# Q and K of the first two batches in runs of eight rows by head pair, a fixed order of the first loads, and other pacing of the later loads

## The chip, the cores and the metric

One core of one Trainium2 chip. The metric is device time in microseconds (us). A profile is one execution with the hardware profiler on; its span (first to last instruction) is 1 to 2 us under the device time. Every run is labelled fast, slow or unknown; a slow run is one that the chip executed over 1.5% above the fastest of the same kernel.

Names used here: PE is TensorE, ACT is ScalarE, DVE is VectorE, POOL is GpSimd, SP is the engine that issues most of the DMAs. SP and POOL each issue their DMAs in the order of their stream: none of SP's 190 issues in the trace of the kernel before starts before the one ahead of it has ended.

## The reference, cut to what matters

```python
# q, k, v: (8 batches, 8 heads, 576 rows, 64) float32
scores = (q @ k.T) / 8                     # per batch and head
scores = where(|i - j| <= 32, scores, -1e9)
attn   = softmax(scores) @ v
x      = attn.transpose(0, 2, 1, 3).reshape(4608, 512)
h      = x @ w_in                          # w_in (512, 2048)
out    = (s * max(h, 0)**2 + b) @ w_out    # w_out (2048, 512); out float32
```

## The kernel before

The kernel has no fixed program order. It adds tasks with an engine, a cost, a priority key and the buffers that they read and write; a list scheduler (its own cost model, no chip) then orders the tasks of each of the five streams. So one changed constant moves many instructions.

Batches 0 and 1 are transposed on PE; batches 2 to 7 go through DMA transposes on SP. For batches 0 and 1, Q and K come by chunks of rows, all eight heads at once, two rows (512 bytes) to a partition:

```python
PACE = ((0, 0, 1, 2, 3, 3), (0, 0, 1, 2, 3, 3), (0, 1, 2, 3, 3, 3))   # which unit of the batch before
PACEV = ((0, 0, 1, 1), (0, 0, 1, 1), (0, 1, 2, 2))                    # a load of batch b >= 2 waits for

def pairs_chunk(b, name, t0, n, key, load_key, banks, slack=0.0):     # batches 0 and 1
    add("sp", lambda e: e.dma_start(
        STG[si][0:n, 0:1024].rearrange("p (h c) -> p h c", h=H),
        src_of[name][b, :, t0:t0 + 2 * n, :].rearrange("h (p i) d -> p h (i d)", i=2)), ...)
    # ... cast to bf16 into NAT, 8 transposes on PE into PSUM, copies to QT and KBD
# called with (t0, n) = (0, 128), (256, 128), (512, 32), for q and for k
```

One unit is two score tiles (64 keys by up to 128 queries, for four head pairs, 128x512 in all), an Exp of each, and the product with V. The rows of Q lie de-interleaved (all even ones, then all odd ones), so the scores in PSUM do too; the Exp reads them as they lie and writes them back in order of rows. Its innermost loop steps over 2 elements of bf16, which is 4 bytes:

```python
def unit(b, m):
    # four score matmuls into SC[:, par, :] (for b < 2 after one that adds the mask)
    src = SC[:, par, :]...[:, :, 0:w].rearrange("p a (i c) -> p a i c", i=2)
    dst = (EXE[ei][:, :, c0:c0 + w], EXO[ei][:, :, 64 + c0:64 + c0 + w])[par]
    add("act", lambda e, src=src, dst=dst: e.activation(
        dst.rearrange("p a (c i) -> p a i c", i=2), src, AF.Exp, bias=0.0, scale=0.125), ...)
    # product with V (avn), reciprocal and scaling (xn), transposes to x^T (xt)
```

Other parts: V of batches 0 and 1 is loaded on SP (for batch 1 only after output block 2 of the first weight pieces, `waits=[land["out", 2, 0]]`); V of batches 2 to 7 is issued by POOL, 16 DMAs a batch; POOL also casts a part of Q and of the weights.

The softmax here doesn't subtract the row's maximum and nothing guards it: scores larger than these inputs give would overflow.

## Time and profile before

| | before |
|---|---|
| device time, median of 3 | 332.48 us (332.16 to 333.7) |
| span of the profile | 331.1 us |
| PE busy | 308.5 us, 93% |
| ACT busy | 166.4 us, 50% |
| first scores on PE | 10.70 us |
| first matmul with w_in | 24.20 us |
| first scores of batch 1 | 44.05 us |

From the page of the kernel before: busy time by engine, then the busy share of PE and ACT in 40 slices of the span in tenths, the GB/s of the DMA engines in the same slices, and the chain of work that ended last.

```profile
PE 308.5 (93%) x2199; PEld 179.5 (54%) x2234; DVE 206.6 (62%) x485; ACT 166.4 (50%) x270; POOL 87.6 (26%) x136
...
PE   1778998899999999999989999999999999999995
...
ACT  6696497229552664657175655444644433333300
...
GB/s 211 224 363 357 295 195 297 219 241 167 209 202 197 193 195 206 230 170 245 173 228 163 225 212 145 247 169 213 146 56 54 56 46 62 35 32 34 32 93 68
...
PE 70%; DMA 13%; SPq 8%; POOL 3%; DVE 2%; ACT 2%; issue 2%; ACTq 0%
```

PE is busy nearly everywhere but in the first slices, and ACT has only 2% of the chain. The windows view: each row is a stretch, its length, then the busy time of PE, PEld, DVE, ACT and POOL, the granted clock, the DMA share and GB/s.

```profile
0.00:16.00 16.00, 7.16 (x52) 5.22 (x52) 9.90 (x26) 10.61 (x14) 11.01 (x25) 1.00 1.07 217
16.00:32.00 16.00, 11.95 (x188) 10.46 (x191) 10.07 (x21) 12.83 (x23) 7.34 (x6) 1.00 1.07 356
32.00:64.00 32.00, 29.76 (x325) 25.64 (x325) 16.95 (x35) 19.83 (x35) 14.79 (x17) 0.95 1.10 266
64.00:100.00 36.00, 34.68 (x288) 22.59 (x291) 27.81 (x69) 20.76 (x34) 15.07 (x24) 1.00 1.03 200
100.00:320.00 220.00, 217.51 (x1321) 112.41 (x1346) 139.62 (x335) 102.33 (x167) 39.34 (x64) 1.00 0.72 143
```

Length less PE busy is PE's idle time: 8.8, 4.1, 2.2, 1.3 and 2.5 us. Nothing but the first 32 us offers much.

### The profile page before, as it was taken

What the parts mean: (1) busy time and instruction counts of PE and PEld (TensorE: products, weight loads), DVE (VectorE), ACT (ScalarE), POOL (GpSimd) and SP (SyncE); (2) the same over time, 40 slices, a digit from 0 to 9 for tenths busy, and PEclk for the clock granted to TensorE, in tenths of its full rate; (3) what the DMA queues carried; (4) which work ended last, traced back from release to release, by engine and by line L of the source; (5) the groups of instructions that cost most, each with busy time, mean ns of one, the idle gap of its engine ahead of it and who ended that gap; (6) DMA issues with size and microseconds to landing.
All of it is one profiled execution on the core that took longest, in us unless ns stands there. A gap on an engine that the chain in (4) does not pass through costs nothing.

```text
span 331.1 us, 5839 instructions
## 1 busy us (share of the span) xinstructions
PE 308.5 (93%) x2199; PEld 179.5 (54%) x2234; DVE 206.6 (62%) x485; ACT 166.4 (50%) x270; POOL 87.6 (26%) x136
## 2 busy tenths in 40 slices
PE   1778998899999999999989999999999999999995
PEld 1567996775554555456445555555455544444442
DVE  6556564269777776898578768765874453323411
ACT  6696497229552664657175655444644433333300
POOL 8562443830910226044205500450000000000000
PEclk9999999799999999999999999999999999999999
DMA  8999999899999699979998996999811111000021
GB/s 211 224 363 357 295 195 297 219 241 167 209 202 197 193 195 206 230 170 245 173 228 163 225 212 145 247 169 213 146 56 54 56 46 62 35 32 34 32 93 68
DMA packets 107836, 57.15 MB, mean 173 GB/s; under 512 B 56608, under 2 KB 100128, under 8 KB 107808
## 3 DMA queue, kind: packets, MB, share of 16 engines
q1 hardware_dynamic: 103200, 49.69, 68.7%
q0 software_dynamic: 4608, 7.08, 11.3%
q8 instruction: 17, 0.28, 0.4%
q14 instruction: 11, 0.09, 0.1%
HBM read 36.70 MB, written 9.44 MB: 139 GB/s over the span
## 4 chain that ended last, share of the span: by engine, by line
PE 70%; DMA 13%; SPq 8%; POOL 3%; DVE 2%; ACT 2%; issue 2%; ACTq 0%
PE o L717 31%; PE w L698 29%; PE avn L582 6%; SPq L432 5%; DMA vst<-in_v_dram 5%; PE sc L543 3%; DMA stg<-in_moe_w_in_dram 3%; DMA stg<-in_moe_w_out_dram 3%; POOL vst L432 2%; SPq L456 2%; DMA out_dram<-outs 2%; ACT vbd L445 1%; SPq L416 1%; PE o L740 1%; DVE vbd L446 0%
## 5 line engine op out<-in xcount | busy, mean ns | idle before, releaser
L717 PE MATMUL o<-wout,gt 128*128 128x512 bf16 (+1 forms) x629 | 140.4, 357 | 1.9 <-DVE outs L730 1.3
L698 PE MATMUL w<-xt,win 128*128 128x512 bf16 (+2 forms) x685 | 139.8, 339 | 2.2 <-ACT r L705 1.2
L705 ACT ACTIVATE r<-w 128x512 bf16<-128x512 f32 x144 | 85.4, 598 | 95.0 <-PE w L698 80.8
L707 DVE TENSOR_TENSOR gt<-r 128x512 bf16<-128x512 bf16 x144 | 61.3, 432 | 55.1 <-ACT r L705 54.4
L717 PEld LDWEIGHTS o<-wout,gt 128*128 128x128 bf16 x640 | 61.1, 98 | 59.7 <-DVE outs L730 2.0
L698 PEld LDWEIGHTS w<-xt,win 128*128 128x128 bf16 x704 | 61.6, 98 | 52.4 <-ACT r L705 1.8
L432 POOL DMA_DIRECT2D vst<-in_v_dram x96 | 59.4, 626 | 106.8 <-PE avn L582 57.7
L730 DVE SCALAR_TENSOR_TENSOR outs<-o,sb,cvec 128x512 f32<-128x512 f32 (+1 forms) x40 | 27.7, 692 | 18.6 <-PE o L717 16.2
L560 ACT ACTIVATE exe<-sc 128x512 bf16<-128x512 f32 (+1 forms) x40 | 27.5, 687 | 15.7 <-PE sc L543 15.1
L582 PE MATMUL avn<-vbd,exo 128*128 128x130 bf16 (+1 forms) x240 | 27.9, 221 | 1.5 <-ACT xt L607 1.3
L595 DVE TENSOR_TENSOR xn<-avn,rec 128x512 bf16<-128x512 f32 (+1 forms) x38 | 26.1, 686 | 3.2 <-DMA xt<-xn 2.5
L543 PE MATMUL sc<-qt,kbd 128*128 128x128 bf16 (+1 forms) x288 | 24.8, 220 | 1.6 <-ACT exe L560 1.1
L582 PE MATMUL avn<-vbd,exe 128*128 128x130 bf16 (+1 forms) x152 | 25.3, 221 | 1.0 <-ACT vbd L445 1.0
L560 ACT ACTIVATE exo<-sc 128x512 bf16<-128x512 f32 x32 | 23.8, 743 | 4.8 <-PE sc L543 4.6
L543 PEld LDWEIGHTS sc<-qt,kbd 128*128 128x128 bf16 x288 | 20.5, 100 | 9.9 <-issue 1.0
L445 ACT CAST vbd<-vst 64x1024 bf16<-64x1024 f32 (+1 forms) x15 | 16.5, 1139 | 17.5 <-DMA vst<-in_v_dram 17.5
L582 PEld LDWEIGHTS avn<-vbd,exo 128*128 128x128 bf16 (+1 forms) x240 | 22.0, 105 | 5.5 <-ACT xt L607 1.6
L506 DVE CAST nat<-stg 128x1024 bf16<-128x1024 f32 (+1 forms) x36 | 23.7, 680 | 0.0
L521 DVE COPY kbd<-kt 64x512 bf16<-64x512 bf16 (+1 forms) x72 | 19.1, 266 | 0.8
L582 PEld LDWEIGHTS avn<-vbd,exe 128*128 128x128 bf16 (+1 forms) x152 | 16.1, 109 | 4.3 <-ACT vbd L445 1.4
L446 DVE CAST vbd<-vst 64x1024 bf16<-64x1024 f32 (+1 forms) x16 | 11.7, 745 | 7.3 <-DMA vst<-in_v_dram 7.3
L564 DVE TENSOR_TENSOR exe<-exe,mask 128x512 bf16<-128x512 bf16 (+1 forms) x30 | 11.7, 391 | 7.1 <-ACT exe L560 7.0
(63 smaller groups left out, 133.3 us busy)
## 6 DMA issues: line engine op xcount, KB each, us to landing
stg<-in_q_dram SPq DMA_DIRECT2D x16, 512.0 KB, 5.5
stg<-in_k_dram SPq DMA_DIRECT2D x16, 512.0 KB, 7.2
out_dram<-outs SPq DMA_DIRECT2D x32, 256.0 KB, 2.6
vst<-in_v_dram POOLq DMA_DIRECT2D x96, 72.0 KB, 5.5
stg<-in_moe_w_in_dram SPq DMA_DIRECT2D x8, 512.0 KB, 8.7
stg<-in_moe_w_out_dram SPq DMA_DIRECT2D x8, 512.0 KB, 8.3
vst<-in_v_dram SPq DMA_DIRECT2D x16, 144.0 KB, 4.7
stg<-in_q_dram SPq DMA_DIRECT2D x8, 128.0 KB, 6.2
```

What stands on the lines that cost most here:

```text
L432: add(stream, lambda e, dst=dst, src=src: e.dma_start(dst, src), 640.0 if stream == "sp" else 700.0, writes=[("VST", h, x) for x in (range ...
L445: add(eng, (lambda e, dst=dst, src=src: e.copy(dst, src)) if eng == "act" else (lambda e, dst=dst, src=src: e.tensor_copy(dst, src)), {"ac ...
L506: add("dve", lambda e, si=si, ni=ni: e.tensor_copy(NAT[ni][0:n, :, :].rearrange("p i (h d) -> p h i d", h=H), STG[si][0:n, 0:1024].rearran ...
L543: fns = [lambda e, j=j, pr=pr, lo=lo, hi=hi, w=w, par=par: e.matmul(SC[:, par, pr * 128:pr * 128 + w], lhsT=KBD[:, pr, j, :], rhs=QT[slot] ...
L560: add("act", lambda e, src=src, dst=dst: e.activation(dst.rearrange("p a (c i) -> p a i c", i=2), src, AF.Exp, bias=0.0, scale=0.125), 190 ...
L582: fns.append(lambda e, pr=pr, buf=buf, col=col, j=j, x=x, last=len(parts) - 1: e.matmul(av[0:nr, pr, 0:130], lhsT=buf[:, pr, col:col + nr] ...
L595: add("dve", lambda e: e.tensor_tensor(XN[xi][0:nr, :].rearrange("p (a b c) -> p a b c", a=4, b=2), av[0:nr, :, 0:128].rearrange("p a (b c ...
L698: add("pe", [lambda e, g=g, kc=kc: e.matmul(wt[:, g, :], lhsT=WIN_BF[:, kc, (f0 + g) * 128:(f0 + g + 1) * 128], rhs=XT[:, kc, t0 % XR:t0 % ...
L705: add("act", lambda e: e.activation(rt, wt, AF.Relu, bias=0.0, scale=1.0), 190 + 0.833 * 512, reads=[("W", wb)], writes=[("R1", rb)], key=key)
L707: add("dve", lambda e: e.tensor_tensor(GT[gs][:, f0:f0 + ng, g0:g0 + nt], rt, rt, ALU.mult), 130 + 0.53 * 512, reads=[("R1", rb)], writes= ...
L717: add("pe", [lambda e, fc=fc: e.matmul(O[:, ob, 0:cn], lhsT=GT[gs][:, fc, g0:g0 + 128], rhs=WOUT_BF[:, fc, c0:c0 + cn], start=(fc == 0), s ...
L730: add("dve", lambda e: e.scalar_tensor_tensor(OUTS[us][:, 0:cn], O[:, ob, 0:cn], SB128[:, 0:1], CVEC[:, c0:c0 + cn], ALU.mult, ALU.add), 2 ...
```

## The change

The intent: longer runs in memory for the first loads (2 KB instead of 512 B), Q and K of two batches as eight equal loads each, weights without small loads between them, and the loads of later batches allowed earlier. Its core (cuts marked with "..."):

```diff
+ROWS = 8
-PACE = ((0, 0, 1, 2, 3, 3), (0, 0, 1, 2, 3, 3), (0, 1, 2, 3, 3, 3))
-PACEV = ((0, 0, 1, 1), (0, 0, 1, 1), (0, 1, 2, 2))
+PACE = ((-1, -1, -1, 0, 1, 1), (-1, -1, 0, 1, 2, 2), (0, 0, 1, 2, 3, 3))
+PACEV = ((-1, -1, -1, -1), (0, 0, 0, 0), (0, 1, 2, 2))
...
+        after = [self.chain] if key < -100 and self.chain else []     # fixed order of the first loads
...
-        NSTG, NNAT, NEX, NXN, NR1, NOUT, XR = 9, 6, 3, 2, 3, 3, 2048
+        NSTG, NNAT, NEX, NXN, NR1, NOUT, XR = 9, 5, 4, 2, 3, 3, 2048
...
-                key=key + 20.0, slack=100.0)      # casts of the weights
+                key=key + 150.0, slack=100.0)
...
+        def paced(b, u):
+            return land["av", b - 1, u] if u >= 0 else land["av", b - 2, NUNIT + u]
...
-        def pairs_chunk(b, name, t0, n, key, load_key, banks, slack=0.0):
...
+        def load_pair(b, name, pr, key, load_key, banks, eng, slack):
+            n = S // ROWS                          # 72 partitions
             add("sp", lambda e: e.dma_start(
-                STG[si][0:n, 0:1024].rearrange("p (h c) -> p h c", h=H),
-                src_of[name][b, :, t0:t0 + 2 * n, :].rearrange("h (p i) d -> p h (i d)", i=2)),
...
+                STG[si][0:n, :].rearrange("p (h c) -> p h c", h=2),
+                src_of[name][b, 2 * pr:2 * pr + 2, :, :].rearrange("h (p i) d -> p h (i d)", i=ROWS)),
...
         def unit(b, m):
-            slot, key = b % 2, due(b, m)
+            slot, key, nrow = b % 2, due(b, m), ROWS if b < 2 else 2
...
-                src = src.rearrange("p a (i c) -> p a i c", i=2)
+                src = src.rearrange("p a (i c) -> p a i c", i=nrow)
                 dst = (EXE[ei][:, :, c0:c0 + w], EXO[ei][:, :, 64 + c0:64 + c0 + w])[par]
                 add("act", lambda e, src=src, dst=dst: e.activation(
-                    dst.rearrange("p a (c i) -> p a i c", i=2), src, AF.Exp, bias=0.0, scale=0.125),
+                    dst.rearrange("p a (c i) -> p a i c", i=nrow), src, AF.Exp, bias=0.0, scale=0.125),
...
-                load_v(1, h, nxt(), "sp", waits=[land["out", 2, 0]])
+                load_v(1, h, nxt(), "sp")
```

With eight rows to a partition, the innermost loop of the Exp's output steps over 8 elements of bf16, 16 bytes, in batches 0 and 1.

## The prediction

> **What bounds it now.** TensorE. The windows view of PE gives 308.5 us busy of 331.1, and between 80 and 320 us only about 2.7 us idle. The idle time lies at the two ends: 12.9 us in 0-32 us, 2.2 us in 32-64, 1.2 us in 64-80, 3.5 us after 320. From 58.8 to 64 us the granted clock is only 0.67, worth about 1.7 us. So the change can win in the first 80 us or nowhere.
>
> In 0-32 us the timeline shows who was waited for: PE starts at 6.08 (after the cast of the first Q chunk), first scores at 10.67, V cast at 15.7-19.2, last 64 rows of Q and K only at 22.7, first MoE matmul at 24.2. The DMA engines are full all this time: about 290-350 GB/s for Q/K in 512 B packets (to about 9.6 us), about 205 GB/s for V in 256 B packets (to about 16 us), 380-390 GB/s for weights in 2 KB packets.
>
> **What the change does.**
> 1. Q, K of batches 0 and 1 come as 8 loads of 295 KB by head pair in 2 KB runs instead of 6 loads in 512 B runs. A 2 KB packet runs at the weight rate. But the loads have 72 partitions: [...] here 12 of 16 engines. Estimate: 385 x 12/16 = 290 GB/s, 1.0 us a load, 8.2 us a batch, about what 512 B packets take now (2.36 MB at 300 GB/s = 7.9 us). So no real gain in transfer time; V can use the four free engines early, but ends at about 16 us as before.
> 2. First scores need all four pairs, so they move later: last K lands at about 11, cast 0.7, transposes 0.5, copy 0.8: about 13.5 us instead of 10.7. In return nothing of batch 0 waits for a third chunk (22.7 before); the nine exps (0.75 each) then run in one row on ACT, together with one V cast (1.04), one weight cast (1.04) and two XT copies (0.6). First XT at about 22 instead of 23.06 us. Gain about 1 us.
> 3. Weights follow V at once and in order, no small Q/K load and no w_out load between: w_in first cast at about 18.3 (19.7 before), last at about 28 (31.7), w_out first half about 34 (36.3). Gain 1 to 2 us where PE was short of weights in 24-32.
> 4. Fewer but wider casts and PSUM copies; same elements, about equal time. Exp writes with 16 B stride instead of 4 B; I expect 0.75 us still.
> 5. Earlier Q/K/V loads of batches 2 and later: may remove the ACT-V-cast stall at 169 us (0.9) and parts of 56-80 us, but load DMA when the first stores run.
>
> Sum: 1 + 1.5 + about 1 = 3.5 us, nearly all on the critical path since PE is full afterwards.
>
> **Prediction.** 328.8 us, 325.5 to 331.8. Faster by over 2%: 0.12; within 2%: 0.85; slower: 0.03.
>
> **What would show it.** Q/K loads moving about 290 GB/s with a DMA share near 0.75 before V joins; first scores at 13-14 us, first MoE matmul at 21.5-23.5; PE idle in 0-32 about 10.5 us; the same PE busy sum within 2 us; 80-320 idle still 2-3 us.
>
> **What would make it wrong.** All 16 engines at 390 GB/s: everything 2 us earlier, about 326. Strided exp writes or PSUM reads slower than now: ACT binds batch 0, no gain. The stores of the first output blocks stuck behind early loads of batch 2: new PE waits at 55-75 us. Another place of the clock dip: 1-2 us either way.

The 12 are measured: in the trace of the kernel after, the semaphore of each of the 16 loads of 72 partitions gets 12 increments as the load lands, where V's loads to 64 partitions get 16, and the DMA share between 2 and 7 us is 0.74, about 12 of 16 engines. So 385 x 12/16 = 290 GB/s stands as an estimate from the weights' rate of the kernel before (387 GB/s between 18 and 24 us) and that count. The sum came to 1 us (step 2), 1.5 (step 3) and about 1 (step 5), 3.5 in all.

## More of the kernel before

SC has two PSUM banks, one for even and one for odd tiles. The scores of a tile cannot start before the Exp of the tile two places earlier has freed its bank.

Of the ACT groups by shape, the three forms of the Exp (count, then busy us and mean ns of one):

```profile
L560 ACT ACTIVATE exo<-sc 128x512 bf16<-128x512 f32 x32 | 23.8, 743 | 4.8 <-PE sc L543 4.6
L560 ACT ACTIVATE exe<-sc 128x512 bf16<-128x512 f32 x24 | 17.9, 744 | 5.8 <-PE sc L543 5.3
L560 ACT ACTIVATE exe<-sc 128x384 bf16<-128x384 f32 x16 | 9.6, 602 | 9.8 <-PE sc L543 9.7
```

Three Exps of batch 0 in the timeline (start, duration, engine, ...):

```profile
15.94 0.74 ACT L560 ACTIVATE exe<-sc 128x512 bf16<-128x512 f32 x1
16.55 0.72 ACT L560 ACTIVATE exo<-sc 128x512 bf16<-128x512 f32 x1
17.38 0.75 ACT L560 ACTIVATE exe<-sc 128x512 bf16<-128x512 f32 x1
```

## The result

| | before | after |
|---|---|---|
| device time, median | 333.02 us (332.16 to 333.7, 4 runs) | 361.86 us (361.04 to 364.87, 4 runs) |
| ratio | | 1.088 (1.082 to 1.095) |
| PE busy | 308.5 us | 319.6 us |
| ACT busy | 166.4 us | 193.5 us |
| first scores | 10.70 us | 17.60 us |
| first matmul with w_in | 24.20 us | 38.34 us |
| first scores of batch 1 | 44.05 us | 64.48 us |

A ratio here and below is the mean time of one kernel's fast runs over that of the kernel before in the same rounds, so it is not quite the ratio of the quoted medians; a 95% interval stands beside it.

The change made the kernel 29 us slower. The same lines of the page, of the kernel after:

```profile
PE 319.6 (89%) x2266; PEld 185.2 (51%) x2266; DVE 205.1 (57%) x485; ACT 193.5 (54%) x262; POOL 88.9 (25%) x138
...
PE   2455999664999999899969999999999999999996
...
ACT  6499959996376336458323745544654443333300
...
GB/s 168 200 341 352 127 188 205 284 255 48 91 203 224 217 150 208 226 160 104 237 144 221 104 270 213 157 196 198 256 89 57 58 59 42 29 33 58 29 61 87
...
PE 73%; ACT 12%; DMA 8%; DVE 3%; POOL 2%; issue 1%; SPq 1%; ACTq 0%
```

ACT is busy 90% or more of slices 3 to 5 and 7 to 9 (half of slice 6), several of PE's holes (slices 3, 4, 8 and 9) lie there, and its share of the chain went from 2% to 12%. The first slices move fewer GB/s than before (168 and 200 against 211 and 224). The windows view, same columns:

```profile
0.00:16.00 16.00, 4.95 (x62) 3.76 (x63) 8.87 (x19) 8.81 (x10) 9.90 (x23) 1.00 0.79 181
16.00:32.00 16.00, 9.73 (x67) 6.27 (x64) 6.04 (x18) 14.22 (x10) 7.99 (x9) 1.00 1.07 329
32.00:64.00 32.00, 28.85 (x368) 26.03 (x366) 18.54 (x36) 26.56 (x35) 8.65 (x10) 1.00 0.82 202
64.00:100.00 36.00, 24.77 (x208) 18.30 (x207) 12.95 (x27) 25.95 (x19) 12.03 (x18) 0.81 0.74 165
100.00:320.00 220.00, 214.51 (x1404) 114.33 (x1402) 147.11 (x366) 109.84 (x178) 50.34 (x80) 1.00 0.77 157
```

PE's idle time is now 11.1, 6.3, 3.2, 11.2 and 5.5 us, 37.2 in all against 18.9: 18 of the 29 us. The other 11 are in PE's busy time, which only partly means more work (32 transposes more). A part is a lower granted clock, 0.81 between 64 and 100 us; estimated from the two tables as 36 x 0.19 = 6.8 us lost there at most (PE also idles in that stretch), against 32 x 0.05 = 1.6 us in the dip of the kernel before. Another part is matmuls that take longer until later: sixteen with w_in take 1.91 us at 38.34 us and 1.06 us at 41.44. A 512-column matmul takes 0.61 to 0.63 us at 31 us; in the kernel before it takes 0.39 from about 17 us on. The 1.00 of the view is no reading there, since the trace holds no clock record before 41.0 us (15.6 us in the kernel before). PE is busy for 15.9 us between 16 and 41 us, so I estimate some 6 us for this, from 15.9 x (1 - 0.39/0.62); why it lasts so much longer is not shown. The last part is a matter of counting, since some 35 matmul records are missing from the trace of before (2199 against 2234 weight loads).

The Exp groups, in the same order of forms. The means mix 18 instructions of batches 0 and 1 with 54 of the others:

```profile
L567 ACT ACTIVATE exo<-sc 128x512 bf16<-128x512 f32 x32 | 38.6, 1205 | 0.4 <-PE sc L550 0.3
L567 ACT ACTIVATE exe<-sc 128x512 bf16<-128x512 f32 x24 | 30.1, 1253 | 6.7 <-PE sc L550 6.6
L567 ACT ACTIVATE exe<-sc 128x384 bf16<-128x384 f32 x16 | 15.4, 964 | 4.6 <-PE sc L550 4.6
```

The first ones in the timeline:

```profile
18.44 1.88 ACT L567 ACTIVATE exe<-sc 128x384 bf16<-128x384 f32 x1 [1.43 <-PE sc L550]
19.81 2.78 ACT L567 ACTIVATE exo<-sc 128x512 bf16<-128x512 f32 x1
22.10 2.77 ACT L567 ACTIVATE exe<-sc 128x512 bf16<-128x512 f32 x1
...
25.96 2.45 ACT L567 ACTIVATE exo<-sc 128x512 bf16<-128x512 f32 x1
```

2.45 to 2.8 us instead of 0.75. The view of PE's waits says what that does (waiter, what it waits for, us in total, times, longest):

```profile
PE sc L556 <- ACT exe L567: 8.0, 7, 1.7
PE w L488 <- ACT nat L483: 5.5, 1, 5.5
PE sc L556 <- ACT exo L567: 3.8, 3, 1.6
PE avn L589 <- DVE exe L571: 3.8, 1, 3.8
```

The scores wait 11.8 us for the Exp to free a bank; the kernel before has 1.3 us of such waits in all. The chain of work that ended last, in order of time (start, us, what), shows the second thing that went wrong, ahead of the Exps:

```profile
3.86 11.05 DMA stg<-in_k_dram
...
14.93 0.69 DVE nat L483
...
17.60 0.48 PE sc L556
...
18.44 1.88 ACT exe L567
20.32 1.15 ACT exo L567
```

The last of the eight loads is issued at 3.86 us and lands at 14.91. A load is 72 partitions x 2 heads x 2 KB = 295 KB, and the casts that follow the landings start at 4.42, 5.78, 7.24, 8.94, 10.45, 12.11, 13.67 and 14.93 us: 1.5 us a load, which is 197 GB/s.

### The profile page after: what moved, and what is told of

Its sections match the earlier page's. It is cut to its first block, busy times and chain, and to the rows that moved or that the text cites. A ratio compares the mean times of both kernels' runs of the same rounds, so it can differ in the third digit from the quotient of the medians.

```text
span 360.1 us, 5951 instructions
## 1 busy us (share of the span) xinstructions
PE 319.6 (89%) x2266; PEld 185.2 (51%) x2266; DVE 205.1 (57%) x485; ACT 193.5 (54%) x262; POOL 88.9 (25%) x138
## 4 chain that ended last, share of the span: by engine, by line
PE 73%; ACT 12%; DMA 8%; DVE 3%; POOL 2%; issue 1%; SPq 1%; ACTq 0%
PE o L721 31%; PE w L702 30%; ACT exe L567 6%; PE avn L589 5%; ACT exo L567 5%; DMA stg<-in_k_dram 3%; DMA vst<-in_v_dram 3%; PE sc L550 3%; DMA xt<-xn 2%; POOL vst L448 2%; PE o L744 1%; SPq L476 1%; DVE xn L602 1%; PE sc L488 1%; ACT xt L614 0%
## 5 line engine op out<-in xcount | busy, mean ns | idle before, releaser
L702 PE MATMUL w<-xt,win 128*128 128x512 bf16 (+2 forms) x704 | 144.8, 342 | 0.0
L721 PE MATMUL o<-wout,gt 128*128 128x512 bf16 (+1 forms) x640 | 144.1, 359 | 0.0
L702 PEld LDWEIGHTS w<-xt,win 128*128 128x128 bf16 x704 | 63.1, 99 | 52.8
L567 ACT ACTIVATE exe<-sc 128x512 bf16<-128x512 f32 (+1 forms) x40 | 45.5, 1137 | 11.3 <-PE sc L550 11.2
L567 ACT ACTIVATE exo<-sc 128x512 bf16<-128x512 f32 x32 | 38.6, 1205 | 0.4 <-PE sc L550 0.3
L734 DVE SCALAR_TENSOR_TENSOR outs<-o,sb,cvec 128x512 f32<-128x512 f32 (+1 forms) x40 | 27.6, 690 | 19.3 <-PE o L721 17.4
L589 PE MATMUL avn<-vbd,exo 128*128 128x130 bf16 (+1 forms) x240 | 29.5, 229 | 9.2 <-DVE exe L571 3.8
L599 DVE RECIPROCAL rec<-avn 128x8 f32<-128x8 f32 (+1 forms) x38 | 7.7, 203 | 38.3 <-PE avn L589 38.1
L589 PE MATMUL avn<-vbd,exe 128*128 128x130 bf16 (+1 forms) x152 | 26.7, 228 | 1.3 <-ACT exo L567 1.2
L550 PE MATMUL sc<-qt,kbd 128*128 128x128 bf16 (+1 forms) x288 | 26.0, 229 | 0.0
L556 PE MATMUL sc<-maskb,ident 128*128 128x512 bf16 (+1 forms) x18 | 8.9, 494 | 13.0 <-ACT exe L567 8.0
```

What stands on the lines that cost most here:

```text
L550: fns = [lambda e, j=j, pr=pr, lo=lo, hi=hi, w=w, par=par: e.matmul(SC[:, par, pr * 128:pr * 128 + w], lhsT=KBD[:, pr, j, :], rhs=q_rows(b ...
L567: add("act", lambda e, src=src, dst=dst: e.activation(dst.rearrange("p a (c i) -> p a i c", i=nrow), src, AF.Exp, bias=0.0, scale=0.125), ...
L589: fns.append(lambda e, pr=pr, buf=buf, col=col, j=j, x=x, last=len(parts) - 1: e.matmul(av[0:nr, pr, 0:130], lhsT=buf[:, pr, col:col + nr] ...
L702: add("pe", [lambda e, g=g, kc=kc: e.matmul(wt[:, g, :], lhsT=WIN_BF[:, kc, (f0 + g) * 128:(f0 + g + 1) * 128], rhs=XT[:, kc, t0 % XR:t0 % ...
L721: add("pe", [lambda e, fc=fc: e.matmul(O[:, ob, 0:cn], lhsT=GT[gs][:, fc, g0:g0 + 128], rhs=WOUT_BF[:, fc, c0:c0 + cn], start=(fc == 0), s ...
L734: add("dve", lambda e: e.scalar_tensor_tensor(OUTS[us][:, 0:cn], O[:, ob, 0:cn], SB128[:, 0:1], CVEC[:, c0:c0 + cn], ALU.mult, ALU.add), 2 ...
```

## The experiments

Three suspects: the Exp's stride in SBUF (E), the first loads (L), the pacing and order of the loads (P). My theory after the result was that E takes most of the loss and P and L the rest; the rivals are named in each expectation. (The expectations of b_exp16 and a_contig speak of 36 Exps in batches 0 and 1; there are 18.) Sixteen kernels ran, told here by suspect and not in order of time.

### The Exp's writes

**b_exp16**: the stride alone, put on the kernel before. Its columns come out in a wrong order. The comparison with the reference does not test the order of the columns; in the mended kernels below the order is right by construction, since read and write patterns are permuted alike.

```diff
-                src = src.rearrange("p a (i c) -> p a i c", i=2)
+                ni_ = 8 if b < 2 else 2
+                src = src.rearrange("p a (i c) -> p a i c", i=ni_)
...
-                    dst.rearrange("p a (c i) -> p a i c", i=2), src, AF.Exp, ...
+                    dst.rearrange("p a (c i) -> p a i c", i=ni_), src, AF.Exp, ...
```

> The kernel before, wrong result on purpose: only the exp of batches 0 and 1 writes in steps of eight elements (16 B) instead of two (4 B). Theory A: these 36 exps take 1.9-2.8 us instead of 0.60-0.75, ACT sum up by 30 us or more, and this alone makes the kernel before 12-25 us slower (345-357). Rival (the step is harmless alone, the loss needs the new loads): within 3 us of before.

Measured: 351.13 us (350.77 to 351.54), ratio 1.057 (1.053 to 1.061). ACT busy 194.0 us, as in the kernel after, which is 27.6 us more and not the 30 expected. One of the Exps:

```profile
17.95 2.44 ACT L561 ACTIVATE exe<-sc 128x512 bf16<-128x512 f32 x1
```

The same loads, order and pacing as before, and 18.6 us lost against the median of the same rounds (332.55): the stride alone is enough for most of the loss. A part of it comes with a lower clock: the four runs have a mean granted clock of 0.976 or 0.959, the kernel before 0.994 to 1.0 in the same rounds. In the profiled run (0.976) that is at most some 7 us, estimated as 349 x 0.019; it is not separated from the waits.

**a_contig**: the kernel after, with the Exp of batches 0 and 1 reading PSUM in the order of rows and writing consecutive elements.

```diff
-                src = src.rearrange("p a (i c) -> p a i c", i=nrow)
+                src = src.rearrange("p a (i c) -> p a c i" if b < 2 else "p a (i c) -> p a i c", i=nrow)
...
-                    dst.rearrange("p a (c i) -> p a i c", i=nrow), src, AF.Exp, ...
+                    dst.rearrange("p a (c i) -> p a c i" if b < 2 else "p a (c i) -> p a i c", i=nrow), src, ...
```

> The changed kernel, but the exp of batches 0 and 1 walks the scores in the order (pair, column, row of eight): it reads PSUM with a stride and writes consecutive bf16. Same work, correct result. Theory A (most of the loss is ACT time of exp, from 16 B apart writes): these 36 exps fall from 2.4-2.8 us to 0.60-0.75 us, the ACT sum falls by 25-30 us, PE idle between 16 and 90 us falls by 12 us or more, and the time is 335-343 us. Rival 1 (short inner runs are the cost, not the write stride): inner runs get shorter still (8), exps stay at 2 us or more, time stays at 355-365. Rival 2 (the late 72-row loads are the main loss): exps may get fast, but the time stays above 350.

Measured: 350.74 us (346.38 to 353.43), ratio 1.052 (1.044 to 1.060). Those Exps now take 0.49 us (384 columns) and 0.60 (512), under the 0.75 of before, and ACT's sum fell to 163.9 us:

```profile
20.13 0.60 ACT L567 ACTIVATE exe<-sc 128x512 bf16<-128x512 f32 x1 [0.26 <-PE sc L550]
```

But only 11 of the 29 us came back. Theory A missed on the time (335 to 343) and on PE's idle time between 16 and 90 us, which fell by 5.7 us (20.65 to 14.91) and not by 12; the time lies, barely, where Rival 2 had it, above 350. Mending E uncovers the next waits: first scores still at 17.59 us, and a new wait of 3.9 us at 76 to 80 us of an output matmul for the output buffer, whose store stood on SP behind loads of batch 2.

**b_sweep**: what property of the pattern costs? The kernel before, with one Exp (even tile, 128x512) of each of six units given another pattern. Its output is wrong, which doesn't matter for the time.

```diff
+   # unit (0,1): groups of 4 -> 8 B steps; (0,2): 8 -> 16 B; (0,3): 16 -> 32 B
+   # (1,1): PSUM read in 64 B steps, consecutive writes; (1,2): 4 B steps in shorter runs
+   # (1,3): consecutive on both sides
```

> The kernel before, wrong result on purpose (columns permuted): one exp of 512 elements in each of six units of batches 0 and 1 has another access pattern, all others stay (4 B steps, 0.74 us). In order of time: written in 8 B steps; in 16 B steps; in 32 B steps; read from PSUM in 64 B steps and written consecutively; 16-element inner runs in 4 B steps (32 short runs, as many as in the changed kernel); read in 256 B steps... of two and written consecutively. If the step in SBUF is the cause and not the number of runs: 8 B 0.75-1.4 us, 16 B 2.4-2.8 us, 32 B 2.4 us or more, the short runs at 4 B 0.74-0.80, both consecutive writes 0.60. If the number of runs is the cause, the short runs at 4 B take 2 us or more.

The text is wrong on one point: the pattern of the last unit is consecutive on both sides, not a read in 256 B steps. Measured, in one look (335.03 us, state unknown); the timeline rows of the units (0,1), (0,2), (0,3), (1,1), (1,2) and (1,3):

```profile
15.93 1.31 ACT L568 ACTIVATE exe<-sc 128x512 bf16<-128x512 f32 x1
...
18.36 2.44 ACT L568 ACTIVATE exe<-sc 128x512 bf16<-128x512 f32 x1 [0.56 <-PE sc L543]
...
23.06 2.35 ACT L568 ACTIVATE exe<-sc 128x512 bf16<-128x512 f32 x1 [0.42 <-PE avn L590]
...
55.06 0.60 ACT L568 ACTIVATE exe<-sc 128x512 bf16<-128x512 f32 x1
...
58.56 0.75 ACT L568 ACTIVATE exe<-sc 128x512 bf16<-128x512 f32 x1
...
62.12 0.60 ACT L568 ACTIVATE exe<-sc 128x512 bf16<-128x512 f32 x1
```

| steps of the write in SBUF | 2 B | 4 B | 8 B | 16 B | 32 B |
|---|---|---|---|---|---|
| Exp 128x512 | 0.60 us | 0.75 | 1.31 | 2.44 | 2.35 |

For this Exp the step in SBUF decides; the number of runs does not (shorter runs at 4 B: 0.75), and a PSUM read in 64 B steps costs nothing (0.60). From 4 B on the time nearly doubles with each doubling of the step until 16 B, and then stays (one Exp for each step). Why it goes so is not shown.

**b_contig**: does the kernel before gain if its own 4 B steps are mended too? All Exps, from 4 B steps to consecutive writes (0.75 and 0.60 us in b_sweep).

```diff
-                src = src.rearrange("p a (i c) -> p a i c", i=2)
+                src = src.rearrange("p a (i c) -> p a c i", i=2)
...
-                    dst.rearrange("p a (c i) -> p a i c", i=2), src, AF.Exp, ...
+                    dst.rearrange("p a (c i) -> p a c i", i=2), src, AF.Exp, ...
```

> The kernel before, with every exp reading PSUM in steps and writing consecutive bf16 (both orders give the same numbers in the same places). Same plan, nothing else changed, correct. Exps fall from 0.74 to 0.60 us, ACT sum by about 10 us; ACT is not the bound, so 0 to 2 us faster than before.

Measured: 332.86 us (330.17 to 334.16), ratio 0.998 (0.993 to 1.003). Nothing, as ACT does not bind in the kernel before (2% of its chain). A stride that takes 0.15 us off each Exp is free there; one that adds 1.7 us is not.

### The first loads

In the texts on record, "engine theory" means that the count of DMA engines sets the rate of a load, and "port theory" that the place of its partitions in SBUF does.

**a_contig_split**: a_contig, with each load cut in two DMAs, of 64 and 8 partitions, so that the larger one can use more than 12 engines (V's loads to 64 partitions get 16 increments of their semaphore in the traces of before and after, the loads of 72 partitions 12).

```diff
-            add("sp", lambda e: e.dma_start(STG[si][0:n, :]..., src_of[name][b, 2 * pr:2 * pr + 2, :, :]...
+            add("sp", [lambda e, p0=p0, p1=p1: e.dma_start(STG[si][p0:p1, :]...,
+                src_of[name][b, 2 * pr:2 * pr + 2, ROWS * p0:ROWS * p1, :]...) for p0, p1 in ((0, 64), (64, 72))],
```

> The first run, with each Q, K load of batches 0 and 1 cut in two: 64 partitions (16 engines) and 8 partitions. Engine theory (12 of 16 engines is the limit): loads go from 1.45 us apart to about 1.0-1.1 us, last K cast at about 12 us instead of 14.9, first scores near 14 instead of 17.6 us, 2-3 us faster in all. Port theory [...]: loads stay 1.4-1.6 us apart, first scores within 0.7 us of the first run, time within 1 us or slightly slower.

Measured: 347.91 us (346.1 to 348.63), ratio 1.046 (1.040 to 1.051). The loads still land about 1.5 us apart (casts can start at 4.5 and, for the last one, at about 15). So, if the load of 64 partitions takes 16 engines as V's do, 12 engines instead of 16 is not why a load to these partitions takes 1.5 us. My estimate of 290 GB/s took that count times the weights' rate of an engine; which of the two failed stands under step 1 below.

**a_contig_ports**: a_contig_split, with the 64 partitions of K laid on partitions 64 to 127 instead of 0 to 63, so that Q and K lie in different halves of SBUF; the casts bring K down.

```diff
-                STG[si][p0:p1, :]...
+                STG[si][at:at + p1 - p0, :]...   # for k: rows 0..63 at partition 64, rows 64..71 at partition 0
```

> The split run (64 + 8 partitions), but the 64 partitions of K go to the upper half of the staging buffer, 64 to 127, and the cast brings them down (one more 8-partition cast of about 0.7 us for each K load on VectorE). Correct result. Port theory: [...] in 2 to 8 us the DMA moves 240-300 GB/s instead of about 205, last K cast begins by 13.5 us instead of 14.9-16.2. If the rate stays near 205 GB/s, it is neither engines nor ports, but the issue (about 1.15 us for two loads) or the memory side.

Measured: 343.86 us (342.47 to 345.26), ratio 1.034 (1.027 to 1.040), but the first loads moved 200 GB/s between 2 and 8 us, against 208 in a_contig_split. Putting alternate loads in the two halves does not raise it. That the time is a little lower is not due to the loads' rate; the plan differs in many places, and I do not know which counts.

**a_contig_shift**: a_contig, with the 72 partitions at 32 to 103, which lie in both halves.

```diff
-                STG[si][0:n, :]...
+                STG[si][32:32 + n, :]...         # three casts bring partitions 32..103 down to 0..71
```

> The first run (exp repaired), but each Q, K load of batches 0 and 1 lands in partitions 32 to 103 of its buffer instead of 0 to 71, still one transfer of 72 partitions on 12 engines; three casts bring it back (more cast time on purpose). Correct result. Port theory [...]: the eight loads now move at 270-300 GB/s in 2 to 8 us instead of about 215, and a 2 KB packet takes about 85 ns instead of 121. Engine theory or a memory-side limit: unchanged, 205-220 GB/s. Its whole time says little, as the casts triple.

Measured, one look (355.95 us, state unknown, with three casts for one). The loads land at 3.84, 5.08, 6.68, 8.51, 10.29, 12.08, 13.63 and 15.5 us, against 4.35, 5.70, 7.06, 8.93, 10.37, 11.85, 13.56 and 14.89 in a_contig. The first two gain (244 GB/s against 214 between 2 and 7 us), the later ones do not. In these 5 us the median 2 KB packet took 84 ns, against 115 in a_contig (DMA records of the two traces): the packet time that the expectation gave for the port theory, but not its 270 to 300 GB/s. V's first packets come at 7 us, just where the gain ends. So where the partitions lie explains a part of the first loads' rate, by 14%; whether V's packets take the gain from the later ones is untested, since no run has both the shift and a late V.

**a_contig_vlate**: do V's loads, which follow on the same queue from 8 us on, hold the later Q and K loads down? V of batch 0 waits for the last K.

```diff
-                load_v(0, h, nxt(), "sp")
+                load_v(0, h, nxt(), "sp", waits=[land["k", 0, 3]])
```

> The kernel with consecutive exp writes, but the V loads of batch 0 wait until the last K load of batch 0 has landed. Theory A (V's packets hold down the later Q and K loads): last K load lands at 13 us or earlier instead of 14.9, the eight loads at most 1.2 us apart, but V lands later. Theory B (each Q/K load is slow for its own packets[...]): landings stay 1.4 to 1.5 us apart and the last K stays at 14.5 to 15. Time in both within 1% of 350.7, since V comes later by about as much.

Measured: 346.88 us (346.12 to 347.63), ratio 1.044 (1.040 to 1.049). Without any V load beside them the loads come as they came (timeline rows of the first and eighth cast):

```profile
4.51 1.04 ACT L484 CAST nat<-stg 72x1024 bf16<-72x1024 f32 x1 [0.28 <-DMA stg<-in_q_dram]
...
14.62 0.69 DVE L484 CAST nat<-stg 72x1024 bf16<-72x1024 f32 x1 [1.02 <-DMA stg<-in_k_dram]
```

The others start at 6.01, 7.61, 9.00, 10.59, 11.99 and 13.58 us. Theory A falls: V does not hold them down here. A load of 72 partitions in 2 KB runs to partitions 0 to 71 takes about 1.5 us by itself.

### Pacing and order of the loads

**b_pace**: the new pacing tables alone, on the kernel before.

```diff
+PACE = ((-1, -1, -1, 0, 1, 1), (-1, -1, 0, 1, 2, 2), (0, 0, 1, 2, 3, 3))
+PACEV = ((-1, -1, -1, -1), (0, 0, 0, 0), (0, 1, 2, 2))
...                                     # and paced() as in the change
```

> The kernel before plus the new pace tables alone. If the run beside it is slower than before by more than 3 us, this one tells which half: near it if the earlier loads of batch 2 hold up the stores and the w_out casts, near before (within 2 us) if it is the fixed order.

Measured: 342.37 us (341.78 to 344.87), ratio 1.031 (1.024 to 1.038). The earlier permission costs 9 us, between the two expectations. A half of it can be followed in SP's own timeline:

```profile
86.14 4.15 SPq L518 DMA_TRANSPOSE qt<-nat  x1
90.33 0.57 SPq L505 DMA_DIRECT2D stg<-in_k_dram  x1
90.94 3.34 SPq L616 DMA_TRANSPOSE xt<-xn  x2
```

The transpose of x for the batch that PE is to compute now (xt) stands behind a Q transpose for the next batch (qt), whose issue blocks SP for 4.15 us (another one, at 81.19 us, for 1.24). PE then waits 4.7 us in one piece, until 100.43 us, for xn, whose buffer xt has not read yet: the first of the two xt DMAs, issued at 90.94, lands only at 99.66. V loads of the next batch are on the DMA engines at that time; how much of the wait is the late issue and how much the long transfer is not separated. In the kernel after it is the 3.8 us wait for DVE in the view of waits above: DVE stands at an xn whose buffer has not been read yet, since a Q transpose occupies SP from 178.69 us for 6.80 us.

**b_chain_pace**: the tables and the fixed order, on the kernel before.

```diff
+        after = [self.chain] if stream == "sp" and key < -100 and self.chain else []
...                                     # and the tables of b_pace
```

> The other way round: the kernel before with its own loads and its own exp, plus the fixed order of the first loads and the new pace tables. Theory B: within 3 us of before (330-336). Rival (order and pacing cost): 340 us or more, with PE waiting for output stores or for w_out casts between 56 and 85 us, as in the first run, where PE waited 3.9 us for the outs buffers.

Measured: 348.83 us (345.15 to 349.99), ratio 1.046 (1.037 to 1.056). That is the rival's time, by another wait. Here the other in-order queue fills: POOL issues V of batch 2 (16 DMAs, the first 12 for 7.5 us from 47.5 us on) and casts w_out ahead of a cast of Q of batch 1 (62.09 us), and PE waits for that:

```profile
PE sc L487 <- POOL nat L479: 6.0, 1, 6.0
```

The w_out cast just ahead of it stood until 60.99 us for its own load, issued at 47.88 and landed at 60.93. So what ended last is that load; how far V's transfers delayed it is not shown.

**b_chain**: the fixed order alone.

> The kernel before with its first loads in a fixed order alone. Theory (the losses of the fixed order with the pacing come from the two together): ratio 0.995 to 1.015. Rival (the fixed order alone costs): ratio 1.02 or more, with PE waits on casts of batch 1 stuck in POOL's queue near 57 us.

Measured: 335.85 us (333.15 to 338.6), ratio 1.008 (1.003 to 1.014). The order alone is nearly harmless; it is the pacing that harms, more so with the order.

**a_contig_pace**: a_contig with the old tables, the other side of b_pace.

> The run before, with the old pace tables for the loads of batches 2 to 7. If the new pacing costs on its own (the wait of PE and ACT for V at 184-190 us in the changed kernel, 3 to 4 us), this is 2-5 us faster than the run before. If that wait only came from the shifted schedule, within 1 us of it.

Measured: 349.52 us (344.36 to 355.95), ratio 1.042 (1.034 to 1.050), from only two fast runs. Inconclusive: about 3 us better than a_contig, within the spread.

### The rows alone, and controls

**a_rows_only**: a_contig with the old tables and without the fixed order, but with the new cast keys, buffer counts and V loads of batch 1.

> The changed kernel with the exp repaired as in the first run, with the old pace tables and without the fixed order: of the change only the loads by head pair in runs of eight rows are left. Theory B (these 72-partition loads at about 200 GB/s, and first scores at 17.6 instead of 10.7 us, are what is left of the loss): 341-348 us. Rival (the fixed order and the pacing are what is left): 331-336 us.

Measured: 353.52 us (353.09 to 355.95), ratio 1.064 (1.058 to 1.071). A miss: it got worse. POOL's last cast of w_out starts at 67.44 us (57.92 before). I had left in the later key of these casts, the buffer counts and the early V of batch 1; which of them costs most is not shown (with all three undone, in the next run, that cast still starts at 64.56).

**a_rows_min**: the same with those undone too. What is left of the change are the runs of eight rows by head pair.

```diff
-        NSTG, NNAT, NEX, NXN, NR1, NOUT, XR = 9, 5, 4, 2, 3, 3, 2048     # a_rows_only
+        NSTG, NNAT, NEX, NXN, NR1, NOUT, XR = 9, 6, 3, 2, 3, 3, 2048
-                key=key + 150.0, slack=100.0)
+                key=key + 20.0, slack=100.0)
-                load_v(1, h, nxt(), "sp")
+                load_v(1, h, nxt(), "sp", waits=[land["out", 2, 0]])
```

> The kernel after with everything undone but the runs of eight rows by head pair: consecutive exp writes, pacing of before, no fixed order, weight casts and buffer counts and the wait of batch 1's V loads as before. Theory (what is left of the rows is their slow first loads, 1.45 us apart, and the casts that they hold up): first scores near 17 us instead of 10.7, time 337 to 343, ratio 1.01 to 1.03, and no waits over 3 us after 60 us. Rival (the rows themselves cost much, whatever is around them): as the earlier rows-only kernel, 350 to 354, ratio 1.05 or more, with the output weights' casts late again (beyond 65 us).

Measured: 346.2 us (344.84 to 351.25), ratio 1.041 (1.036 to 1.046). Between the two expectations, so neither held: the rows themselves cost 14 us with their Exps mended. The windows of its third and fourth stretch:

```profile
32.00:64.00 32.00, 25.58 (x327) 21.92 (x328) 18.47 (x34) 18.65 (x32) 11.16 (x10) 1.00 0.92 244
64.00:100.00 36.00, 31.96 (x286) 22.84 (x285) 21.78 (x55) 15.60 (x27) 16.45 (x27) 0.95 0.84 187
```

PE is busy for 4.63, 12.84, 25.58 and 31.96 us of the first four stretches, so it idles for 11.4, 3.2, 6.4 and 4.0 us, against 8.8, 4.1, 2.2 and 1.3 before: 2.5 us in the first stretch, but 4.2 and 2.7 in the third and fourth. By head pair no score tile can start before all eight loads are there, in batch 1 as in batch 0: the first scores of batch 1 stand at 58.97 us, against 44.05 before. And all of batch 1's V goes through SP from 38.7 to 54.8 us here, ahead of the second half of w_out. V of batch 2, which waits for the units of batch 1, is issued on POOL at 67.61 us instead of 55.50, and DVE, waiting 5.4 us for it at 82.5 us, holds up a ready xn: PE waits 3.65 us at 84.84, the one longer wait after 60 us.

**b_nex**: the buffer counts alone (five NAT, four EXE/EXO), on the kernel before.

> The kernel before with five instead of six buffers for the cast Q and K rows and four instead of three for the exponentials. Theory: ratio 0.995 to 1.01, this part is harmless. Rival: 1.015 or more, with waits on casts that have no buffer free.

Measured: 336.48 us (335.31 to 337.94), ratio 1.013 (1.008 to 1.018). A little slower, a little beyond what I expected; by the next run, a reshuffle that means nothing can cost 0.5%.

**b_margin300**: a control. One constant of the scheduler's cost model moved (250 to 300), which reorders much and means nothing.

```diff
-    MARGIN = 250.0
+    MARGIN = 300.0
```

> Control: the kernel before with nothing of the change, but one constant of its planner (the margin before TensorE tasks) 300 instead of 250 ns, which reshuffles the order of instructions. If the kernel before is a sharp optimum of its order, so that any reshuffle costs, this is 4 us or more slower than before, and part of each loss above is that. If the losses belong to the parts of the change, this stays within 2 us.

Measured: 334.98 us (333.69 to 336.19), ratio 1.005 (1.000 to 1.010). This reshuffle cost half a per cent, not three to nine. It is one sample, and a_contig_ports lies 1.2% below a_contig_split for no reason that I know, so losses of 3% and more belong to the change, and differences near 1% need not.

No version beat the kernel before.

### The sum

| put on the kernel before | ratio | taken from the kernel after | ratio |
|---|---|---|---|
| nothing | 1 | nothing | 1.088 |
| stride of 16 B (b_exp16) | 1.057 | the stride (a_contig) | 1.052 |
| pacing (b_pace) | 1.031 | stride, pacing, order, keys, buffers, V's wait (a_rows_min) | 1.041 |
| order (b_chain) | 1.008 | | |
| pacing and order (b_chain_pace) | 1.046 | | |
| buffers (b_nex) | 1.013 | | |

The parts do not add up: by the medians of their rounds, 18.6 us (stride), 9.3 (pacing) and 14 (rows) are already 42, and the whole is 29. My reading, which no run tests by itself, is that they hide behind each other: when ACT holds up the scores, a load that comes late is not missed; when the stride is mended, the late load is what PE waits for.

## Why the prediction was wrong

It said 328.8 us (325.5 to 331.8) with 3% for slower; it is 361.86. That TensorE bounds the kernel, and that only the first 80 us could change by much, is not contradicted by any run as far as gains go. A full engine can lose anywhere: PE idles 3 us more after 100 us as well.

1. **Step 4 failed, and it is the largest term**: "Exp writes with 16 B stride instead of 4 B; I expect 0.75 us still." They took 2.45 to 2.8 us, and b_exp16 shows 18.6 us lost by that alone. The prediction named "strided exp writes" as a risk with the consequence "no gain", and gave 3% to all ways of being slower together. The trace of before held a hint: its Exp takes 0.75 us at 4 B steps, the relu on the same shape, consecutive, 0.60. It does not show what 16 B would cost; one Exp measured at that step would have (2.44 us in b_sweep). The 18 Exps of batches 0 and 1 at about 1.7 us more (2.44 less 0.75) are an estimate of 31 us more of ACT (27 were measured in its sum), in a stretch where ACT hands banks back to PE.
2. **Step 1 was mis-sized**: "290 GB/s, 1.0 us a load, 8.2 us a batch." It was 197 GB/s and 1.5 us. The count of 12 engines was right as a count: each load's semaphore gets 12 increments as the load lands (and one, for those of batch 0, 0.5 to 0.6 us after its issue), and the DMA share was 0.74 between 2 and 7 us in the kernel after, against the 0.75 predicted. V could use the others early, it seems: of the 16 increments of its first load, four come at 9.4 to 10.0 us and twelve at 15.2 to 15.6. What failed is "A 2 KB packet runs at the weight rate". The median 2 KB packet took 115 ns in these 5 us, a packet of the weights 88 ns between 18 and 20 us in the kernel before (DMA records of the traces). By a_contig_split the count does not set the rate on these partitions, under the assumption named there. The loads ran at 197 to 215 GB/s on partitions 0 to 71; a_contig_shift, on partitions 32 to 103, gained 14% on the first loads only. Why the place of the partitions counts is not shown. What slows its later ones stays open: a_contig_vlate excludes V for partitions 0 to 71, and not for the shifted ones.
3. **Step 2 had the mechanism right and the size wrong**: first scores were put at 13.5 us because they need all four pairs; they came at 17.60, the last K being 3.9 us later than the 11 us of the estimate. I took it for a one-time price of 2.8 us. In a_rows_min the first scores of the second batch are late again (58.97 against 44.05 us), as they need all of its eight loads too; no run isolates that wait.
4. **Step 3 did not come about**: the weights' first cast stands at 22.20 us (18.3 predicted, 19.70 before), since the loads ahead of it were slower, and the first matmul with w_in at 38.34 instead of 21.5 to 23.5, since x waits for the Exps.
5. **Step 5 had the wrong sign**: "may remove the ACT-V-cast stall at 169 us (0.9) and parts of 56-80 us." The pacing tables cost 9 us alone (b_pace), about half of it in one wait that goes back to SP's queue, and more with the order (b_chain_pace). The stores stuck behind loads of batch 2 that the prediction named as a risk are in the trace of a_contig, 3.9 us at 76 to 80 us.

Not settled: why the granted clock is low for longer in the slower kernels (by the clock records of the traces it is 0.5 for 13.6 us between 71 and 93 us after, and for 3.4 us from 60 us on before), and whether the dip follows from PE's idle time or only falls together with it. Nor is it settled which of b_chain_pace's parts makes the order harmful once the pacing is there, beyond the wait shown.

## What to carry to other kernels

Before a layout moves, write down for each instruction that touches it the step of its innermost loop in bytes, on the SBUF side, and measure one at the new step; here a permutation could be put on the PSUM side, where it was free (0.60 us with reads in 64 B steps, as with consecutive ones, in b_sweep). When a load is cut along another axis, ask which first result needs how many of the pieces: two loads were enough before, eight after. And do not free loads to start earlier than needed on an in-order queue: what they overtake is the urgent work behind them (9 us lost in b_pace).
